# A bounded load ring, block-end states scaled in PSUM, and small zero matmuls at the start of TensorE, in a fused retention and feed-forward kernel

## The chip, the cores and the metric

The kernel runs on one core of one Trainium2 chip. The metric is the device time of one execution in microseconds. Before the change, five runs took 306.62, 307.52, 307.97, 311.42 and 312.94 us, with a median of 307.97 us. All times inside an execution are counted from the start of the span of the profiled execution.

## The reference

The inputs are q, k and v of shape (batch 8, heads 8, sequence 576, head size 64) and two weight matrices, all in float32. What is computed is a decayed causal product without softmax, then a feed-forward layer with a leaky ReLU:

```python
scores = (1/8) * q @ k.T                      # per batch and head, 576 x 576
ret    = scores * where(i >= j, gamma_h ** (i - j), 0)
x      = (ret @ v) laid out as 4608 tokens x 512
h      = x @ w_in                             # 512 x 2048
out    = maximum(0.01 * h, h) @ w_out         # 2048 x 512
```

gamma_h is 1 - 2^(-5-h) for head h.

## The kernel before

**Tiles.** The 4608 tokens are cut into 36 units of 128 tokens. A unit holds two chunks of 64 tokens; a batch has nine chunks, so units 4, 13, 22 and 31 join the last chunk of one batch with the first of the next. Per unit, q and v are scaled by powers of gamma and cast to float16 (`cast_q`, `cast_v`), and k is cast by ScalarE (`cast_k`). The scaling runs on VectorE for units 0 to 5 and on GpSimd from unit 6 (`NEARLY`). q and k are transposed on TensorE for units 0 to 8 (`transposes`, line 184, copied out of PSUM at line 190 by ScalarE for k and, from unit 4, VectorE for q), and by a DMA on SP's queue from unit 9 (`NPE`).

**Retention.** `scores(u)` makes, in one PSUM tile `sc`, the k-q products inside each chunk and the 64x64 state that each chunk adds (lines 203 and 212). `masks(u)` multiplies the products by the causal mask into SBUF. `states(u)` adds the new state to the running one on VectorE (line 243). At the last chunk of each 256-token block the sum goes first to an SBUF tile `stmp` and is then multiplied by gamma^256 (line 245). `state_copy(u)` casts the state to float16. `outputs(u)` (and `outputs_acc` for units 0 to 3) multiplies masked products by v and states by q in the PSUM tile `ot`; ScalarE and VectorE bring the result to `xT`, the transposed activations. The pools of `sc` and `ot` each hold one buffer.

**Feed-forward.** `g1_blocks(g)` makes, for a group of 256 tokens, blocks of eight matmuls (line 425) and a leaky ReLU on ScalarE (line 432). `g2_blocks` multiplies by w_out (line 448) and stores the rows through SP's queue; `g2_wide` (line 493) does the same for the first four 128-token tiles at once, in sixteen blocks.

**Order.** The order of instructions on every engine is that of the calls, written out by hand for units 0 to 8 (lines 513 to 629), and from there by `run`, which spreads steps of the retention evenly between blocks of the feed-forward. The scheduler adds only the semaphore waits. `keep_warm(n)` puts n matmuls of zeros of full size on TensorE at four places of the start.

**Loads.** k of unit 0 comes through SP's queue. All other loads of units 0 to 11 and both weight matrices are issued by GpSimd, in one queue and in this order: units 0 to 3, w_in in eight parts of half the partitions, a quarter of w_out, unit 4, a quarter of w_out, and, after some of the feed-forward's calls, unit 5, two quarters of w_out, and units 6, 7 and 8. Units 9, 10 and 11 come later in GpSimd's order, each ahead of the scaling of unit 6, 7 or 8; so a load that waits holds up the scaling behind it. The weights are cast from float32 to float16 on the way. GpSimd's DMAs use eight semaphores in turn (99 to 106 in the trace), and each DMA waits for the one eight places ahead of it to land. Loads from unit 12 on go through SP's queue.

The functions that the diff touches, with the line numbers of the profile:

Of the kernel before, what the change touches and what calls it, by code (L numbers as in the profile page):

```python
# [9 lines left out]
FP = mybir.dt.float32  # L10
F16 = mybir.dt.float16
# [6 lines left out]
def kernel(  # L18
# [23 lines left out]
    nc = tc.nc  # L42
    B, H, S, D = q.shape
    NT, DM = out.shape
    DFF = moe_w_in.shape[1]
    P = 128
    CH = 64
    BLK = 256
    NP = H // 2
    NF = DFF // P  # L50
    TOK = 512
    XR = NT // 2

    gamma = 1.0 - 2.0 ** (-5.0 - np.arange(H, dtype=np.float64))
    scale = 1.0 / np.sqrt(D)
# [22 lines left out]
    const_pool = ctx.enter_context(tc.tile_pool(name="const", bufs=1))  # L78
    ld_pool = ctx.enter_context(tc.tile_pool(name="ld", bufs=5))
    a_pool = ctx.enter_context(tc.tile_pool(name="ap", bufs=4))  # L80
# [3 lines left out]
    sc_pool = ctx.enter_context(tc.tile_pool(name="scp", bufs=1, space=PSUM))  # L84
    ot_pool = ctx.enter_context(tc.tile_pool(name="otp", bufs=1, space=PSUM))
    h_pool = ctx.enter_context(tc.tile_pool(name="hpp", bufs=2, space=PSUM))
# [15 lines left out]

    xT = const_pool.tile([P, NP, XR], F16, name="xT")
    w_in16 = const_pool.tile([P, NP, DFF], F16, name="w_in16")
    w_out16 = const_pool.tile([P, NF, DM], F16, name="w_out16")
# [15 lines left out]
    def half(i):  # L121
        return slice(CH * i, CH * i + CH)

    def kind(u):
        return kinds.index(tuple(c % CPB for b, c in units[u]))

    def load(u, x, eng):
        t = ld_pool.tile([P, H, D], FP, name=f"t32_{x}")
        t32[u, x] = t
        (b0, c0), (b1, c1) = units[u]  # L130
        src = (q, k, v)[x]
        parts = [(t, b0, c0, P)] if b0 == b1 else [(t[0:CH], b0, c0, CH), (t[CH:P], b1, c1, CH)]
        for dst, b, c, n in parts:
            eng.dma_start(  # L134
                out=dst, in_=src[b, :, CH * c : CH * c + n, :].rearrange("h t d -> t h d")
            )

    def loads(u, eng):
        for x in (1, 0, 2):
            load(u, x, eng)  # L140

    def cast_k(u):
        qk16[u] = b_pool.tile([P, 2, H, D], F16, name="qk16")
        nc.scalar.copy(out=qk16[u][:, 1], in_=t32[u, 1])  # L144

    def scaled(u, x, out):
        (nc.vector if u < NEARLY else nc.gpsimd).tensor_tensor(  # L147
            out=out,
            in0=t32[u, x],
            in1=tab_sb[:, kind(u), x // 2, :].unsqueeze(2).to_broadcast([P, H, D]),  # L150
            op=MUL,
        )

    def cast_q(u):
        scaled(u, 0, qk16[u][:, 0])
        if u >= NPE:
            qkT[u] = b_pool.tile([P, 2, NP, P], F16, name="qkT")
            nc.sync.dma_start_transpose(
                out=qkT[u].rearrange("p x c t -> p (x c) t"),
                in_=qk16[u].rearrange("t x h d -> t (x h d)"),  # L160
            )

    def cast_v(u):
        v16[u] = b_pool.tile([P, H, D], F16, name="v16")
        scaled(u, 2, v16[u])

    def casts(u):
        if u >= NU:
            return
        cast_k(u)  # L170
        cast_q(u)
        cast_v(u)

    def transposes(u, pool=None):

        qkT[u] = b_pool.tile([P, 2, NP, P], F16, name="qkT")
        if pool is None:
            trs = [y_pool.tile([P, NP, P], F16, name="yps") for x in range(2)]
        else:
            both = pool.tile([P, 2, 2 * NP, P], F16, name="sc")  # L180
            trs = [both[:, x, 0:NP, :] for x in range(2)]
        for x in (1, 0):
            for p in range(NP):
                nc.tensor.transpose(  # L184
                    trs[x][:, p, :],
                    qk16[u][:, x, 2 * p : 2 * p + 2, :].rearrange("t h d -> t (h d)"),
                    ident,
                )
        for x in (1, 0):
            (nc.scalar.copy if x or u < 4 else nc.vector.tensor_copy)(  # L190
                out=qkT[u][:, x], in_=trs[x]
            )
# [35 lines left out]
    def states(u, copy=True):  # L228

        st = sc_tiles[u][:, :, 1]  # L230
        s32 = a_pool.tile([P, 2, NP, CH], FP, name="s32")
        st32[u] = s32
        for j, (b, c) in enumerate(units[u]):
            if c == CB - 1:
                nc.vector.memset(s32[:, j], 0.0)
                continue
            ends_block = c % CPB == CPB - 1
            dst = a_pool.tile([P, NP, CH], FP, name="stmp") if ends_block else s32[:, j]
            if c == 0:
                nc.vector.tensor_copy(out=dst, in_=st[:, j])  # L240
            else:
                prev = s32[:, 0] if j else st32[u - 1][:, 1]
                nc.vector.tensor_tensor(out=dst, in0=st[:, j], in1=prev, op=ADD)  # L243
            if ends_block:
                nc.vector.tensor_tensor(
                    out=s32[:, j], in0=dst,
                    in1=gblk_sb.unsqueeze(2).to_broadcast([P, NP, CH]), op=MUL,
                )
        if copy:
            state_copy(u)  # L250

    def state_copy(u):
        st16[u] = a_pool.tile([P, 2, NP, CH], F16, name="st16")
        (nc.scalar.copy if u < NACT else nc.gpsimd.tensor_copy)(out=st16[u], in_=st32[u])  # L254
# [7 lines left out]
    def outputs_acc(u):  # L262
# [4 lines left out]
        for r in range(2):  # L267
# [11 lines left out]
            for j in range(2):  # L279
                if u == 0 and j == 0:  # L280
                    continue
                for h in (r, r + 4, r + 2, r + 6):
# [6 lines left out]
                    )  # L289
        t0 = P * u % XR  # L290
        nc.scalar.copy(
# [3 lines left out]
    def outputs(u):  # L295
# [15 lines left out]
        for j in range(2):  # L311
            for s in range(2):
                for o in range(2):
                    for g in range(2):
# [6 lines left out]
                        )  # L321
        t0 = P * u % XR
        tmp = a_pool.tile([P, NP, P], FP, name="own")
# [12 lines left out]
    FQ = DFF // 4  # L336

    def load_w_in(f):
        fs = slice(f * FQ, (f + 1) * FQ)
        rows = moe_w_in.rearrange("(o c k) f -> o k c f", o=2, k=CH)  # L340
        for o in range(2):
            nc.gpsimd.dma_start(out=w_in16[half(o), :, fs], in_=rows[o][:, :, fs])

    def load_w_out(c):
        nc.gpsimd.dma_start(
            out=w_out16[:, 4 * c : 4 * c + 4, :],
            in_=moe_w_out[c * FQ : (c + 1) * FQ, :].rearrange("(c k) f -> k c f", k=P),
        )
# [5 lines left out]
    idle = const_pool.tile([P, TOK], F16, name="idle")  # L354
    nc.vector.memset(idle, 0.0)

    def keep_warm(n):

        t = h_pool.tile([P, 1, TOK], FP, name="hps")
        for _ in range(n):  # L360
            nc.tensor.matmul(out=t[:, 0, :], lhsT=idle[:, 0:P], rhs=idle, start=True, stop=True)  # L361

    load(0, 1, nc.sync)
    load(0, 0, nc.gpsimd)
# [48 lines left out]
    def g1_blocks(g):  # L413

        tok, t0 = sizes[g], starts[g]
        nf = TOK // tok

        def block(fb):
            if fb == 0:
                g_tiles[g] = g_pool.tile([P, NF, tok], F16, name=f"gt{tok}")  # L420
            hps = h_pool.tile([P, nf, tok], FP, name="hps")
            for f in range(nf):
                fc = fb * nf + f
                for c in range(NP):
                    nc.tensor.matmul(  # L425
                        out=hps[:, f, :],
                        lhsT=w_in16[:, c, fc * P : (fc + 1) * P],
                        rhs=xT[:, c, t0 % XR : t0 % XR + tok],
                        start=(c == 0),
                        stop=(c == NP - 1),  # L430
                    )
            nc.scalar.activation(  # L432
                out=g_tiles[g][:, fb * nf : (fb + 1) * nf, :], in_=hps,
                func=mybir.ActivationFunctionType.Lrelu,
            )

        return [lambda fb=fb: block(fb) for fb in range(NF // nf)]
# [73 lines left out]
                g1[g][m]()  # L511

    g1 = [g1_blocks(g) for g in range(3)]
    casts(0)
    transposes(0)
    cast_k(1)
    scores(0)
    masks(0)
# [47 lines left out]
    def some(a, b):  # L566
        for m in range(a, b):
            wide[m]()

    g2 = g2_blocks(2)  # L570

    def more(blocks, a, b):
        for m in range(a, b):
            blocks[m]()
# [6 lines left out]
    scores(4)  # L581
    masks(4)
    states(4)
    some(5, 6)
    transposes(5, sc_pool)
    some(6, 8)
    outputs(4)
    some(8, 9)
    scores(5)
# [17 lines left out]
    casts(8)  # L607
    more(g1[2], 1, 3)
    state_copy(6)
    more(g1[2], 3, 4)  # L610
    transposes(7, sc_pool)
    more(g1[2], 4, 5)
    outputs(6)
    loads(12, nc.sync)
    casts(9)
# [4 lines left out]
    states(7, copy=False)  # L620
    more(g1[2], 7, 8)
    state_copy(7)
    casts(10)
    loads(14, nc.sync)
    more(g2, 0, 2)
    outputs(7)
    more(g2, 2, 3)
    transposes(8, sc_pool)
    more(g2, 3, 5)
    run(ends[4], g1_blocks(3), g2[5:])  # L630
    for g in range(4, NG):
        run(ends[g + 1], g1_blocks(g), g2_blocks(g - 1))
    g2 = g2_blocks(NG - 1)
    run(ends[NG], g2[:4])
    for a, b in ((0, 3 * P), (3 * P, DM)):
        y = y_pool.tile([P, DM], FP, name="yps")
        for f in range(NF):
            nc.tensor.matmul(  # L638
                out=y[:, a:b],
                lhsT=g_tiles[NG - 1][:, f, P : 2 * P],  # L640
                rhs=w_out16[:, f, a:b],
                start=(f == 0),
                stop=(f == NF - 1),
# [34 lines left out]
```

## Time and profile before

| What | Value |
|---|---|
| median of five runs (lowest, highest) | 307.97 us (306.62, 312.94) |
| profiled execution: device time | 306.62 us |
| profiled execution: span from first to last instruction | 304.8 us |
| TensorE matmuls busy | 291.8 us (96% of the span) |
| TensorE weight loads busy | 197.9 us (65%) |
| ScalarE busy | 139.7 us (46%) |
| GpSimd busy, without DMA issues' waits | 117.8 us (39%) |
| VectorE busy | 109.5 us (36%) |
| read from and written to HBM | 36.81 MB and 9.44 MB |

The profile is that of one execution. A matmul's busy time includes its way through the array, so TensorE can be shown busy while its clock is at half speed. A line of the timeline gives the start, the duration of the whole group, the engine, the line in the code, the operation, the tiles, how many instructions the group joins, and in brackets how long the engine was idle before it and what ended that. "PEld" is TensorE loading weights.

### The profile page before, as it was taken

The page shows a single profiled execution, that of the slowest core. Times are in us where ns is not written, and L with a number is a line of the kernel's source. Part 1 is how long each engine was busy: PE and PEld are TensorE (multiplying, and loading weights), DVE is VectorE, ACT ScalarE, POOL GpSimd, SP SyncE. Part 2 cuts the span into 40 slices and gives each one's busy share as a digit, 9 for nine tenths or more (in the row PEclk, how much of TensorE's full clock was granted, in tenths as well). Part 3 has the DMA queues.
Part 4 walks back from the last instruction along what each step waited for, and adds up shares of the span by engine and source line. Part 5 has one row for each costly group of instructions (what it writes and reads, how often), then busy time and mean ns, then how long its engine had stood idle before and what let it go on. Part 6 is the DMA issues. An engine that isn't in the chain of part 4 may idle for free.

```text
span 304.8 us, 9364 instructions
## 1 busy us (share of the span) xinstructions
PE 291.8 (96%) x4120; PEld 197.9 (65%) x4120; DVE 109.5 (36%) x210; ACT 139.7 (46%) x242; POOL 117.8 (39%) x142
## 2 busy tenths in 40 slices
PE   1799999999999999999999999999999999999995
PEld 1478744866766666666666666666666666666653
DVE  2750145344542425252525243424333334341001
ACT  4666634855644444444535353535353534343320
POOL 8943959944533333333333333333333330000000
PEclk9999999999999999999999999999999999999999
DMA  7999998999999997977876777767622220000111
GB/s 192 254 187 236 238 279 257 291 217 217 228 204 228 237 229 175 201 162 183 153 186 161 184 173 169 173 169 178 166 73 69 71 71 37 37 37 34 50 56 69
DMA packets 117368, 49.73 MB, mean 163 GB/s; under 512 B 106128, under 2 KB 110608, under 8 KB 117328
## 3 DMA queue, kind: packets, MB, share of 16 engines
q1 hardware_dynamic: 109760, 35.60, 50.2%
q0 software_dynamic: 7136, 13.37, 18.6%
q8 instruction: 32, 0.52, 0.7%
q10 hardware_dynamic: 432, 0.17, 0.3%
q14 instruction: 8, 0.07, 0.1%
HBM read 36.81 MB, written 9.44 MB: 152 GB/s over the span
## 4 chain that ended last, share of the span: by engine, by line
PE 93%; DVE 3%; DMA 1%; ACT 1%; issue 1%; POOL 0%; POOLq 0%; ACTq 0%
PE hps L425 41%; PE yps L448 36%; PE sc L203 3%; PE hps L493 2%; PE yps L493 2%; PE sc L212 2%; PE ot L305 2%; PE ot L316 2%; DMA t<-in_q_dram 1%; PE yps L638 1%; PE yps L184 1%; DVE s L221 1%; PE hps L361 1%; PE sc L184 1%; PE ot L272 1%
## 5 line engine op out<-in xcount | busy, mean ns | idle before, releaser
L425 PE MATMUL hps<-xT,w_in 128*128 128x256 f16 x1152 | 146.2, 273 | 0.0
L432 ACT ACTIVATE gt<-hps 128x512 f16<-128x512 f32 x144 | 86.0, 597 | 126.9 <-PE hps L425 126.8
L425 PEld LDWEIGHTS <-w_in 128*128 128x128 f16 x1152 | 112.2, 98 | 38.1
L448 PE MATMUL yps<-w_out,gt 128*128 128x512 f16 x496 | 126.6, 380 | 0.0
L254 POOL CAST st<-s 128x512 f16<-128x512 f32 x28 | 17.1, 610 | 139.2 <-DVE s L243 69.7
L448 PEld LDWEIGHTS <-gt 128*128 128x128 f16 x496 | 46.2, 98 | 33.9
L328 DVE TENSOR_TENSOR xT<-ot,own 128x512 f16<-128x512 f32 x32 | 22.1, 692 | 77.3 <-ACT own L324 77.3
L458 DVE COPY osb<-yps 128x512 f32<-128x512 f32 x31 | 21.2, 685 | 74.0 <-PE yps L448 74.0
L147 POOL TENSOR_TENSOR qk<-t,cs 128x512 f16<-128x512 f32 x30 | 31.3, 1043 | 0.1
L147 POOL TENSOR_TENSOR v<-t,cs 128x512 f16<-128x512 f32 x30 | 31.3, 1042 | 0.0
L221 DVE TENSOR_TENSOR s<-sc,cs 128x512 f16<-128x512 f32 x36 | 24.6, 683 | 8.9 <-PE sc L212 8.9
L144 ACT CAST qk<-t 128x512 f16<-128x512 f32 x36 | 22.2, 621 | 0.9 <-DMA t<-in_k_dram 0.9
L324 ACT COPY own<-ot 128x512 f32<-128x512 f32 x32 | 18.8, 586 | 7.7 <-PE ot L316 5.9
L243 DVE TENSOR_TENSOR s<-sc,s 128x256 f32<-128x256 f32 x40 | 16.8, 420 | 0.7
L203 PEld LDWEIGHTS <-qkT 64*64 64x64 f16 x576 | 8.1, 111 | 10.9 <-issue 7.8
L134 POOL DMA_DIRECT2D t<-in_q_dram x13 | 11.3, 871 | 4.5 <-DVE qkT L190 2.5
L203 PE MATMUL sc<-qkT 64*64 64x64 f16 x576 | 11.9, 203 | 1.2 <-ACT qkT L190 0.9
L134 POOL DMA_DIRECT2D t<-in_k_dram x12 | 10.4, 864 | 4.6 <-DMA t<-in_k_dram 2.3
L184 PEld LDWEIGHTS <-qk 128*128 128x128 f16 x72 | 5.5, 115 | 9.9 <-ACT qk L144 4.7
L134 POOL DMA_DIRECT2D t<-in_v_dram x13 | 11.1, 854 | 1.8 <-DMA w_in<-in_moe_w_in_dram 1.6
L184 PE MATMUL yps<-ident,qk 128*128 128x128 f16 x32 | 4.5, 309 | 7.5 <-ACT qk L144 4.7
L212 PE MATMUL sc<-v,qk 64*64 64x64 f16 x576 | 11.2, 198 | 0.0
(43 smaller groups left out, 146.1 us busy)
## 6 DMA issues: line engine op xcount, KB each, us to landing
out_dram<-osb SPq DMA_DIRECT2D x35, 256.0 KB, 2.3
t<-in_k_dram SPq DMA_DIRECT2D x22, 256.0 KB, 3.6
t<-in_q_dram SPq DMA_DIRECT2D x21, 256.0 KB, 3.9
t<-in_v_dram SPq DMA_DIRECT2D x21, 256.0 KB, 4.4
t<-in_q_dram POOLq DMA_DIRECT2D x11, 256.0 KB, 4.7
t<-in_v_dram POOLq DMA_DIRECT2D x11, 256.0 KB, 4.9
t<-in_k_dram POOLq DMA_DIRECT2D x10, 256.0 KB, 5.5
w_in<-in_moe_w_in_dram POOLq DMA_DIRECT2D x8, 256.0 KB, 9.4
```

What stands on the lines that cost most here:

```text
L134: eng.dma_start(out=dst, in_=src[b, :, CH * c : CH * c + n, :].rearrange("h t d -> t h d"))
L144: nc.scalar.copy(out=qk16[u][:, 1], in_=t32[u, 1])
L147: (nc.vector if u < NEARLY else nc.gpsimd).tensor_tensor(out=out, in0=t32[u, x], in1=tab_sb[:, kind(u), x // 2, :].unsqueeze(2).to_broadca ...
L203: nc.tensor.matmul(out=a[half(j), g, 0, p, :], lhsT=qkT[u][half(g), 1, p, half(j)], rhs=qkT[u][half(g), 0, p, half(j)], start=True, stop=T ...
L212: nc.tensor.matmul(out=a[half(g), j, 1, p, :], lhsT=qk16[u][half(j), 1, 2 * p + g, :], rhs=v16[u][half(j), 2 * p + g, :], start=True, stop ...
L221: nc.vector.tensor_tensor(out=s16s[u], in0=sc_tiles[u][:, :, 0], in1=mask_sb.unsqueeze(1).unsqueeze(1).to_broadcast([P, 2, NP, CH]), op=MUL,)
L324: nc.scalar.copy(out=tmp.rearrange("q c (j t) -> q c j t", t=CH), in_=own.rearrange("q j c t -> q c j t"),)
L328: nc.vector.tensor_tensor(out=xT[:, :, t0 : t0 + P].rearrange("q (s g) t -> q g s t", g=2), in0=far, in1=tmp.rearrange("q (s g) t -> q g s ...
L425: nc.tensor.matmul(out=hps[:, f, :], lhsT=w_in16[:, c, fc * P : (fc + 1) * P], rhs=xT[:, c, t0 % XR : t0 % XR + tok], start=(c == 0), stop ...
L432: nc.scalar.activation(out=g_tiles[g][:, fb * nf : (fb + 1) * nf, :], in_=hps, func=mybir.ActivationFunctionType.Lrelu,)
L448: nc.tensor.matmul(out=y_cur[g, tb], lhsT=g_tiles[g][:, f, tb * P : (tb + 1) * P], rhs=w_out16[:, f, :], start=(f == 0), stop=(f == NF - 1),)
L458: nc.vector.tensor_copy(out=osb, in_=y_cur[g, tb])
```

## The change

Four things change.

1. GpSimd's loads pass through `ring(size, at)`. It keeps a list of the loads issued, with their size in float32 bytes. Before a load that would bring the sum over 11 x 256 KB (2.75 MB), GpSimd copies one element of the oldest load's destination to a scratch tile, which waits for that load to land, and takes it off the list, until the new one fits.
2. At the end of a 256-token block, the sum of states is written back to its place in the PSUM tile `sc`, and is multiplied by gamma^256 from there. The tile `stmp` is gone.
3. `small_ones(60)` puts 60 matmuls of zeros, 64x64 by 64x64, ahead of everything else on TensorE, and `keep_warm(2)` is added between the transposes and the scores of unit 0.
4. The transposes of units 5, 7 and 8 use the buffer of `ot` in place of that of `sc`, and stand earlier: those of unit 5 before block 5 of `wide`, those of unit 7 one block earlier, and those of unit 8 three blocks of `g2` and `outputs(7)` earlier.

```diff
+    RING = 11 << 18
...
+    landing = []
+    probe = const_pool.tile([P, P], FP, name="probe")
+
+    def ring(size, at):
+        while landing and sum(n for n, _ in landing) + size > RING:
+            x = landing.pop(0)[1]
+            nc.gpsimd.tensor_copy(out=probe[0:1, 0:1], in_=x)
+        landing.append((size, at))
...
+            if eng is nc.gpsimd:
+                ring(H * n * D * 4, dst[0:1, 0, 0:1])
             eng.dma_start(
...
-            both = pool.tile([P, 2, 2 * NP, P], F16, name="sc")
+            both = pool.tile([P, 2, 2 * NP, P], F16, name="sc" if pool is sc_pool else "ot")
...
-            dst = a_pool.tile([P, NP, CH], FP, name="stmp") if ends_block else s32[:, j]
+            dst = st[:, j] if ends_block else s32[:, j]
...
+            ring(CH * NP * FQ * 4, w_in16[CH * o : CH * o + 1, 0, fs.start : fs.start + 1])
             nc.gpsimd.dma_start(out=w_in16[half(o), :, fs], in_=rows[o][:, :, fs])
...
+        ring(P * 4 * DM * 4, w_out16[0:1, 4 * c, 0:1])
         nc.gpsimd.dma_start(
             out=w_out16[:, 4 * c : 4 * c + 4, :],
...
+    def small_ones(n):
+        t = h_pool.tile([P, 1, TOK], FP, name="hps")
+        for i in range(n):
+            nc.tensor.matmul(
+                out=t[half(i % 2), 0, 0:CH], lhsT=idle[0:CH, 0:CH], rhs=idle[0:CH, 0:CH],
+                start=True, stop=True, skip_group_check=True,
+            )
...
+    small_ones(60)
     casts(0)
     transposes(0)
+    keep_warm(2)
     cast_k(1)
...
     states(4)
-    some(5, 6)
-    transposes(5, sc_pool)
-    some(6, 8)
+    transposes(5, ot_pool)
+    some(5, 8)
     outputs(4)
...
     state_copy(6)
-    more(g1[2], 3, 4)
-    transposes(7, sc_pool)
-    more(g1[2], 4, 5)
+    transposes(7, ot_pool)
+    more(g1[2], 3, 5)
     outputs(6)
...
     state_copy(7)
+    transposes(8, ot_pool)
     casts(10)
     loads(14, nc.sync)
     more(g2, 0, 2)
     outputs(7)
-    more(g2, 2, 3)
-    transposes(8, sc_pool)
-    more(g2, 3, 5)
+    more(g2, 2, 5)
```

## The prediction, made before the result was known

> **What bounds the kernel now.** First the page's busy table, the slices and the chain's shares by engine.
>
> ```profile
> PE 291.8 (96%) x4120; PEld 197.9 (65%) x4120; DVE 109.5 (36%) x210; ACT 139.7 (46%) x242; POOL 117.8 (39%) x142
> PE   1799999999999999999999999999999999999995
> DMA  7999998999999997977876777767622220000111
> PE 93%; DVE 3%; DMA 1%; ACT 1%; issue 1%; POOL 0%; POOLq 0%; ACTq 0%
> ```
>
> TensorE sets the end from the second slice on. Only its waits and its clock can give time back; the waits are next.
>
> ```profile
> PE yps L184 <- ACT qk L144: 4.7, 1, 4.7
> PE yps L184 <- DVE qk L147: 2.8, 2, 1.6
> PE sc L184 <- DVE s L240: 0.5, 1, 0.5
> ```
>
> 7.5 us lie at the start, while the first loads land and are cast. The third line is the only wait that the moved transposes can remove. Then the clock, from the timeline: the same two zero matmuls twice, and the places after the start where another engine may come last.
>
> ```profile
> 14.18 1.06 PE L361 MATMUL hps<-idle 128*128 128x512 f16 x2
> 20.70 0.60 PE L361 MATMUL hps<-idle 128*128 128x512 f16 x2
> 25.70 6.50 PE L425 MATMUL hps<-xT,w_in 128*128 128x256 f16 x58
> 43.05 0.61 PE L184 MATMUL sc<-ident,qk 128*128 128x128 f16 x8 [0.48 <-DVE s L240]
> 49.25 1.05 POOL L147 TENSOR_TENSOR qk<-t,cs 128x512 f16<-128x512 f32 x1
> 51.85 0.61 PE L184 MATMUL sc<-ident,qk 128*128 128x128 f16 x8
> 58.15 0.62 ACT L254 CAST st<-s 128x512 f16<-128x512 f32 x1 [0.23 <-ACT gt L432]
> 59.16 0.58 ACT L190 COPY qkT<-sc 128x512 f16<-128x512 f16 x1
> ```
>
> A 512-column matmul advances by 0.427 us at 14 us and by 0.215 us later. The trace's clock record has full speed from 20.43 us for 283.3 us. So everything before 20.43 runs at half speed.
>
> **What the Trainium skill says.** "TensorE: Matmul & The Clock Gate", Part 1: TensorE runs at half clock until one window of about 3.4 us was busy, in windows that run free. The trace agrees: 283.306 us is 83.0 windows of 3.413 us, so the window that opened the gate was 17.02 to 20.43. Part 4 of that page says that transposes do not count as busy. "DMA: Bandwidth & Descriptors", Queues, rings and completion order: each DMA engine takes a queue's descriptors in ring order. The trace agrees: GpSimd's loads land in the order of issue. "VectorE: DVE Perf Modes", Why PSUM operands drop a tier: float32 from PSUM runs at the plain rate; here a sum with a PSUM operand takes 0.41 to 0.42 us and the multiply from SBUF 0.42, so nothing is lost by the source.
>
> **Part 1, small zero matmuls.** Added: 60 of 64x64, alternating column halves. The same pattern (L272) advances in pairs every 0.053 us at half clock, so 60 take 30 x 0.053 = 1.6 us. They start when the zeros are written (VectorE, 1.04 to 1.31) and end near 3.0; the first transposes start at 4.73 when k is cast. They delay nothing. Do they open the gate? Counting array time without transposes in the trace's windows: 13.60 to 17.02 holds two keep-warm matmuls (0.85), scores (0.43) and outputs (0.86): 2.14 of 3.41 us, 63%, and did not open it. 17.02 to 20.43 holds 1.28 + 0.43 + 0.59 = 2.30 us, 67%, and did. So the threshold by this count lies near 65%. The small ones alone reach 1.6/3.41 = 47%. I take: gate not opened early, gain 0. Bound on the gain: if the 60 ran one by one (0.053 each, 3.2 us, 94% of a window that lies right), the start would run warm; what that is worth is the first rival. Bound on the loss: the window that opens the gate passes by only about 2 points, and one window later means 3.41 us at half speed over dense matmuls from 20.7, so +1.7 us.
>
> The added `keep_warm(2)` starts after the transposes of q (last start 6.75 + 0.107 = 6.86) and takes 2 x 0.427 = 0.85, to 7.71; scores of unit 0 wait for ScalarE's copy until 7.69 and started at 7.74. Cover: 0.83 us of wait. Cost 0; without that cover 0.85.
>
> **Part 2, PSUM.** There are 16 such block ends (two in each batch). In place of SBUF the sum is written to PSUM; no row shows VectorE writing PSUM. Between the PSUM copy's 0.36 and the slowest multiply shown (0.73 at 56.55) I take 0.42: no change. What moves is the release of `sc`: after the multiply, not the sum. The tightest place is unit 8: sum until 70.66, multiply 70.68 to 71.10, next scores 71.33; 0.23 us are left, and at 0.73 the wait would be 0.1. Elsewhere a unit is about 5.5 us. Cost 0 to 0.1.
>
> **Part 3, the ring.** From the landing records: the first eleven loads land 0.7 to 1.5 us apart until 14.79, the eight w_in parts at 18.11, 19.41, 20.68, 21.94, 23.22, 25.00, 25.91 and 27.20, the w_out quarters at 29.96, 36.13, 40.87 and 43.78, k, q and v of unit 6 at 44.49, 45.26 and 46.03. They come in order and without a gap, so the transfers are the limit, not the issue. Eight semaphores already hold GpSimd to eight in flight. The ring bites only where eight are more than 2.75 MB. Working it through (w_in part 0.5 MB, w_out quarter 1 MB): the sixth w_in part is issued at 18.5 in place of 14.1, the first w_out quarter at 23.6 for 18.4, the fourth at 36.5 for 33.9, k of unit 7 at 41.3 for 37.6. A load needs 3.4 us from issue to its first landing (q of unit 0: 1.27 to 4.65) when nothing is queued. 18.5 + 3.4 = 21.9 against a first landing of 22.47 before; 27.0 against 27.57; 39.9 against 40.94; for k of unit 7 44.7 against 43.95, 0.7 late, which its casts near 50 and 54 hide. So the transfers stay fed: cost 0, with 0.4 to 1.0 us to spare.
> Behind the waiting GpSimd stand the other loads and then the scaling of unit 6. From k of unit 7 on: nine issues at 0.88 from 41.3, and three one-element copies. No row shows such a copy; a 128x1 MEMSET takes 0.10 and a full CAST 0.61; I take 0.1. 41.3 + 7.9 + 0.3 = 49.5 against 49.25. Scaled q of unit 6 is then there at 50.6 in place of 50.3; TensorE asks for it at 51.85, or 51.35 after the gain below. Cover 0.8 us. The pops of units 9 to 11 add at most 9 x 0.1 over casts that TensorE needs 2 us after they end (unit 7: 54.99 against 57.0).
>
> **Part 4, the transposes.** Unit 5: its start no longer waits 0.48 us for VectorE. But `outputs(4)` now needs `ot`, which is free after the copies: state cast 43.00, k copy 43.70 to 44.29, q copy to 44.74 (VectorE follows ScalarE in every such pair of the trace). TensorE arrives at 41.65 + 0.45 + 3 x 0.865 = 44.7, starts at 44.8, before at 45.32: -0.5.
> Unit 7: from the end of `scores(6)`, now near 54.85, TensorE has 2 x 0.87 + 0.45 + 2 x 0.87 = 3.95 until `outputs(6)`: 58.8. VectorE's chain (0.69 + 0.42 + 0.42 + 0.42) ends near 57.0, the state cast near 57.9 to 58.0 (0.62, behind a leaky ReLU until 57.4), the k copy 58.6, the q copy 59.05. So a new wait of 0.3. Before, the same copies ended at 60.2 and `outputs(6)` at 59.41 waited for neither.
> Unit 8 likewise: `scores(7)` ends at 61.7, VectorE at 63.3, state cast 63.95, k copy 64.6, q copy 65.05; TensorE arrives at 61.7 + 0.87 + 0.45 + 1.73 = 64.75: 0.3.
> Sum -0.5 + 0.3 + 0.3 = +0.1, but the moved blocks are otherwise the same, and at the end of `g2`'s fifth block I get 68.1 against 68.14 before. I take -0.1; bounds -0.5 (no new wait) and +0.5 (the slow multiply in the chain).
>
> **Sum.** 0 + 0 + 0 - 0.1 on the profiled execution: span 304.7, time 306.5. That execution is the fastest of five; 306.62, 307.52 and 307.97 lie together, 307.5 in the middle, and I put the change on that: **307.4 us**, against the median shown of 307.97. About 0.5% (1.5 us) is what a measurement can tell from no change.
>
> **Rivals.** *The gate opens early.* For it: the zero matmuls sit where TensorE is otherwise idle, and one full window is enough. Against: 47%. Worth: the start cannot gain all the half-speed time, because w_in's sixth part lands at 25.00 and the matmuls that need it started at 25.77: 0.77 us, then 0.1 from the transposes. 306.6 - 0.9 = 305.7; against runs whose gate opened one window later (+1.7) more, so about 306.1 on a median of 307.97.
> *The ring starves the transfers* (slower). Place: the waits from the sixth w_in part to k of unit 7, ahead of the scaling of unit 6. Price: what the second w_out quarter's and later landings slip, less the 0.8 us of cover, plus what the following transfers lose. For it: margins of 0.4 to 1 us are thin, and a slowest engine lands 2 to 3 us after the first. Against: 2.5 MB are still queued. From a slip of 2.5 us at the third w_out quarter it decides, +1.7 or more: 309.7, to 311.
> *A later gate*, +1.7, belongs to the forecast's own spread, since before has it too.
>
> **How the numbers follow.** Forecast (nothing much) 0.50, 306.4 to 309.2 on its own; early gate 0.32; starved ring 0.18. Faster by over 0.5%: 0.75 of the early gate and 0.12 of the forecast, 0.30. Slower: 0.9 of the ring, and 0.03 of the forecast, 0.18. The rest 0.52. The range 305.5 to 309.7 leaves out half of the ring's case and a little of each other.
>
> **What would show it.** Right: 512-column zero matmuls at 0.43 us until about 20, full clock from near 20.4; no wait of transposes on VectorE at 43; waits of `ot` on line 190 of some 0.3 us near 59 and 65; w_in's sixth part landing at 25. Wrong: full clock recorded before 10 us; matmuls of line 425 waiting for w_in; the transposes of unit 6 waiting for GpSimd; the landings of w_out more than 1 us later.

## The result, and the profile after

The changed kernel took 310.24 us in the median of 43 runs (308.28 to 313.52). On the same chips the kernel before took 310.73 us in 80 runs (306.62 to 313.47). The ratio is 1.0026, with a 95% interval from 1.0007 to 1.0044. The ratio leaves out runs more than 1.5% above a kernel's own fastest; the fastest run of before is 1.7 us below that of after, so more of before's long runs fall away, and that alone puts the ratio above 1 while the medians stand the other way round. Within 0.5% the two kernels take the same time. But the fastest run became 1.7 us slower (13 of the 80 runs of before lie below the fastest of the 43), and 310.24 lies outside the range of 305.5 to 309.7.

The profiled execution after took 311.7 us, with a span of 309.1 (before 304.8). First the page's busy table, the slices of TensorE and of the DMA engines, and the chain's shares by engine.

```profile
PE 296.9 (96%) x4182; PEld 201.1 (65%) x4182; DVE 110.2 (36%) x210; ACT 139.8 (45%) x242; POOL 124.2 (40%) x181
PE   4799999999889999999999999999999999999995
DMA  7999999899899999959595867676722221000011
PE 89%; DMA 3%; DVE 2%; ACT 2%; issue 1%; SPq 1%; POOL 0%; POOLq 0%; ACTq 0%
```

TensorE still sets the end. GpSimd has 39 instructions more: the copies of the ring. DMA has 3% of the chain in place of 1%, and SP's queue ("SPq") is new in it with 1%. TensorE's waits show where:

```profile
PE yps L197 <- DVE qk L160: 2.4, 2, 1.2
PE sc L216 <- DMA qkT<-qk: 1.9, 2, 1.5
PE yps L197 <- ACT qk L157: 1.8, 2, 1.4
PE hps L382 <- DVE idle L370: 1.4, 1, 1.4
```

The second line is new: scores waited for a transpose made by DMA. The half microsecond that line 184 waited for VectorE is gone. From the timeline, in order of time: the start, the moved transposes of unit 5, the transposes of unit 6, and the wait.

```profile
1.36 1.81 PE L382 MATMUL hps<-idle 64*64 64x64 f16 x60 [1.36 <-DVE idle L370]
20.89 1.04 PE L376 MATMUL hps<-idle 128*128 128x512 f16 x2
21.72 5.47 PE L449 MATMUL hps<-xT,w_in 128*128 128x256 f16 x32
43.84 0.62 PE L197 MATMUL ot<-ident,qk 128*128 128x128 f16 x8
53.52 0.61 PE L197 MATMUL sc<-ident,qk 128*128 128x128 f16 x8
85.71 0.32 PE L216 MATMUL sc<-qkT 64*64 64x64 f16 x16 [1.53 <-DMA qkT<-qk]
```

At 20.89 two full-size zero matmuls still take 1.04 us, which is half speed, and so does most of the group of 32 matmuls of line 449. In the clock record full speed comes at 25.43 us, before at 20.43. The starts of `scores(u)` divide the 4.3 us of longer span:

| start of scores | unit 4 | 5 | 6 | 10 | 11 | 12 | 15 |
|---|---|---|---|---|---|---|---|
| before, us | 41.16 | 46.66 | 54.99 | 75.40 | 81.64 | 87.60 | 112.49 |
| after, us | 43.47 | 48.33 | 56.66 | 77.55 | 85.71 | 92.07 | 116.88 |
| difference | +2.31 | +1.67 | +1.67 | +2.15 | +4.07 | +4.47 | +4.39 |

So the later clock is +2.3, the moved transposes of unit 5 are -0.6, units 6 to 10 lose 0.5 again, and +2.2 come with scores of units 11 and 12, most of it waits for their DMA transposes (1.9). None of the four is a wait of TensorE for GpSimd. Yet the ring had moved GpSimd's work. First GpSimd's timeline of after, then that of before: the third w_out quarter, k of unit 7 and the scaling of q of unit 6.

```profile
33.65 1.35 POOL L132 COPY probe<-t 1x1 f32<-1x1 f32 x6
35.12 0.76 POOL L360 DMA_DIRECT2D w_out<-in_moe_w_out_dram  x1
37.36 0.17 POOL L132 CAST probe<-w_out 1x1 f32<-1x1 f16 x1 [1.49 <-DMA w_out<-in_moe_w_out_dram]
...
43.16 0.17 POOL L132 CAST probe<-w_out 1x1 f32<-1x1 f16 x1 [1.59 <-DMA w_out<-in_moe_w_out_dram]
43.63 0.89 POOL L147 DMA_DIRECT2D t<-in_k_dram  x1 [0.29 <-issue]
...
51.87 1.05 POOL L160 TENSOR_TENSOR qk<-t,cs 128x512 f16<-128x512 f32 x1
```

```profile
33.14 1.53 POOL L345 DMA_DIRECT2D w_out<-in_moe_w_out_dram  x2
...
49.25 1.05 POOL L147 TENSOR_TENSOR qk<-t,cs 128x512 f16<-128x512 f32 x1
```

The scaled q is ready at 52.92, before at 50.31: 2.6 us later. TensorE came for it near 53.7 (53.52, after four transposes of k), because its clock was late too, so 0.8 us were spare. In an execution whose clock opens early, they would not be. The experiments began there.

### The profile page after: what moved, and what is told of

The parts are those of the page before. It is cut to its first block, busy times and chain, and to the rows that moved or that the text cites. A ratio compares the mean times of both kernels' runs of the same rounds, so it can differ in the third digit from the quotient of the medians.

```text
span 309.1 us, 9540 instructions
## 1 busy us (share of the span) xinstructions
PE 296.9 (96%) x4182; PEld 201.1 (65%) x4182; DVE 110.2 (36%) x210; ACT 139.8 (45%) x242; POOL 124.2 (40%) x181
## 4 chain that ended last, share of the span: by engine, by line
PE 89%; DMA 3%; DVE 2%; ACT 2%; issue 1%; SPq 1%; POOL 0%; POOLq 0%; ACTq 0%
PE hps L449 39%; PE yps L472 33%; PE sc L216 3%; PE yps L517 2%; PE hps L517 2%; DMA qkT<-qk 2%; PE sc L225 2%; PE ot L318 2%; PE ot L329 1%; DMA t<-in_q_dram 1%; PE hps L376 1%; PE yps L661 1%; PE yps L197 1%; PE ot L285 1%; SPq L147 1%
## 5 line engine op out<-in xcount | busy, mean ns | idle before, releaser
L449 PE MATMUL hps<-xT,w_in 128*128 128x256 f16 x1152 | 147.9, 275 | 0.0
L329 PE MATMUL ot<-qkT,st 64*64 64x64 f16 x512 | 10.3, 194 | 0.6 <-issue 0.3
L318 PE MATMUL ot<-s,v 64*64 64x64 f16 x512 | 9.8, 194 | 0.2
```

The source lines that it names most:

```text
L449: nc.tensor.matmul(out=hps[:, f, :], lhsT=w_in16[:, c, fc * P : (fc + 1) * P], rhs=xT[:, c, t0 % XR : t0 % XR + tok], start=(c == 0), stop ...
```

## The experiments

Each ratio below is against the kernel before, on the same chip. Times are medians, with the fastest run in brackets.

### One part at a time

`ring_only` is the kernel before with the `ring` calls of the diff alone; `no_ring` is the changed kernel with `RING = 1 << 40`; `start_only` is the kernel before with `small_ones(60)` and `keep_warm(2)`. `fill_before` fills the start with full-size zero matmuls, so that the clock should open early in every execution:

```diff
+            if x and u < 2:            # in transposes, between k and q
+                keep_warm(3 + u)
...
+    keep_warm(7)                       # ahead of casts(0)
...
+    keep_warm(2)                       # after transposes(0)
...
+    keep_warm(1)
     transposes(1)
-    keep_warm(1)
+    keep_warm(2)
```

> The kernel before with the ring alone. Theory A: TensorE's clock opens by chance, early (near 20 us) in about one execution of three and late (23 to 25.5 us) in the others, whatever the change; the ring delays GpSimd's scaling of unit 6 by 2 to 2.6 us, which costs about 1.5 us in executions that open early and little in the others. Then the fastest runs are near 308.2 us in place of 306.6 to 307.5, and the middle is 0.1 to 0.4% above before. Rival B: the moved transposes, which now share the buffer of the outputs, make the loss: then this kernel equals before within 0.1%, its fastest runs included. Rival C: the small matmuls change when the clock opens: then it equals before too.

> The changed kernel with the ring's bound set so high that nothing is held back; all else of the change stays. Theory A: the loss is gone, fastest runs near 306.5 to 307, ratio to before 0.998 to 1.000. Rival B (moved transposes) and rival C (small matmuls): the loss stays, fastest runs near 308.3, ratio 1.002 to 1.003.

> The kernel before with the 60 small matmuls and the two added zero matmuls alone. Theory A and rival B: equal to before within 0.1% with both groups of times, the clock opening near 20 or from 23 to 25.5 us in the trace. Rival C: the early group of times (306.6 to 308) is missing, or the clock opens before 10 us.

> The kernel before with full-size zero matmuls (128x128 by 128x512) in every wait of TensorE from 1.36 to 11 us: 7 ahead of the first transposes, 3 between those of k and q of unit 0, 2 after them, 1 and 4 around those of k of unit 1, one more after unit 1. If the clock opens with the first window of 3.4 us that is full enough of matmuls, it opens between 4.5 and 8.5 us in every execution, and the time is near 305.8 us with little spread: w_in's sixth part still lands near 25.0, so at most 0.8 us are gained on the execution of before at 306.6, but 4 us on its late ones, about 1.3% against before's middle. If the opening hangs on something else, nothing changes.

| kernel | us (fastest) | ratio, 95% | clock full from | scaled q of unit 6 |
|---|---|---|---|---|
| ring_only | 310.23 (308.63) | 1.0004 [0.9976, 1.0032] | 19.35 | 54.25 |
| no_ring | 309.38 (306.54) | 0.9975 [0.9941, 1.0010] | 25.10 | 51.08 |
| start_only | 309.65 (306.40) | 0.9963 [0.9929, 0.9997] | 15.92 | |
| fill_before | 308.62 (306.92) | 0.9966 [0.9940, 0.9992] | 6.82 | |

The medians hardly differ; the fastest runs do. With the ring the fastest is 308.3 to 308.6, without it 306.4 to 306.9. In the profile of `ring_only`, where the clock opened at 19.35, TensorE's timeline has the wait that after's profile missed by 0.8 us:

```profile
54.31 0.40 PE L197 MATMUL sc<-ident,qk 128*128 128x128 f16 x4 [1.65 <-POOL qk L160]
```

`fill_before` opened the clock at 6.82. Its scores of unit 4 began at 40.09, 1.1 us earlier than before's. But TensorE's waits show what followed:

```profile
PE sc L205 <- DMA qkT<-qk: 3.2, 1, 3.2
```

Scores of unit 11 waited 3.2 us for the DMA transpose, and the clock record has half speed from 85.32 to 88.73, one window, soon after it. TensorE came for it about 1 us earlier than in before, and the transpose, issued at 77.48 in both, landed 2.3 us later (83.81 for 81.51). In before it had landed 0.1 us ahead of TensorE, so there was no room for either.

### The transposes' place on SP, and the bound's size

In every steady step SP issues three loads (`loads(n + 7)`) ahead of a transpose (`casts(n + 3)`). `swap_only` turns that round in the kernel before; `fill_swap` has it together with the filled start and without the ring. `fill_after` is the changed kernel with the filled start in place of the 60 small matmuls; `ring_4mb` has a bound of 4 MB.

```diff
+            casts(n + 3)
             if n + 7 < NU:
                 loads(n + 7, nc.sync)
-            casts(n + 3)
```

> The changed kernel, its 60 small matmuls replaced by the full-size zero matmuls of the kernel that opens the clock early: so the clock's chance is taken out, and ring, PSUM and moved transposes stay. Theory A (the ring costs where the start is quick): the transposes of unit 6 wait 2 us or more for GpSimd, no run below 308.3 us, median 309.5 or more, at least 0.9 us over the 308.6 of the same filling without the ring. Rival (ring harmless, its missing fast runs were the clock's chance): no such wait, median at or below 308.6, fastest near 306.5.

> The changed kernel with the ring's bound at 4 MB in place of 2.75 MB: the copies remain, most of the waits for landings go. If the loss is the transfers of w_out starved by the bound: the third quarter of w_out lands near 41 us in place of 43.0, scaled q of unit 6 is there near 51, fastest runs are back near 307, the median at 309.4 as without the ring. If it is the time that GpSimd spends in the copies: scaled q of unit 6 stays near 52 to 53, fastest runs stay at 308.3 or above.

> The kernel before, with one swap in the steady steps: the scaling and DMA transpose of unit n+3 are called before the loads of unit n+7, so that on SP's queue the transpose of unit 11 no longer stands behind three loads. If the wait of the scores of unit 11 for that transpose (0 to 3.2 us in the profiles) is what sets part of the spread, it vanishes: the transpose of unit 11 is issued near 74.5 in place of 77.5 and lands before 79, the clock no longer closes again near 85, and the median falls by 0.5 to 1.5 us to 309 to 310. If the wait only follows from the transfers' total, it stays.

> All that promises a gain together: the changed kernel without the ring's waits, with the full-size zero matmuls at the start, and with the swap of transposes and loads. Clock open by 8.5 us, no wait for GpSimd at unit 6, none for the transpose of unit 11: 305.5 to 306.5 us with a spread below 2 us, 1.3% or more below before's middle. If the wait at unit 11 stays, 308 to 309.

| kernel | us (fastest) | ratio, 95% | clock full from | scaled q of unit 6 |
|---|---|---|---|---|
| fill_after | 311.36 (308.15) | 1.0049 [1.0020, 1.0077] | 4.21 | 51.54 |
| ring_4mb | 309.41 (307.67) | 1.0001 [0.9974, 1.0028] | 24.55 | 51.90 |
| swap_only | 310.19 (306.42) | 0.9995 [0.9956, 1.0035] | 27.93 | |
| fill_swap | 306.26 (305.20) | 0.9909 [0.9875, 0.9943] | 6.60 | 50.61 |

The filled start makes the changed kernel slower. Its profile has a wait of 0.9 us for q of unit 6, then one of 2.9 us for the transpose of unit 11, then a window at half speed (86.13 to 89.55):

```profile
PE sc L218 <- DMA qkT<-qk: 2.9, 1, 2.9
...
PE sc L197 <- POOL qk L160: 0.9, 1, 0.9
```

`ring_4mb` keeps 34 of the 39 copies. Its third w_out quarter landed at 41.52 in place of 43.04, and its median is that of `no_ring` (309.41 and 309.38), as expected if the waits for landings cost most; its fastest run, 307.67, came only part of the way to the 307 expected.
The same start together with the swap and without the ring is faster than both kernels: `fill_swap` is 4.3 us below before and 4.0 below after, by the medians. Its profile has no wait at unit 11. The swap alone gains nothing that can be measured, where 0.5 to 1.5 us were expected; its profiled execution was one of its longest (312.42 us), with the latest clock of all and an idle stretch of 1.7 us on TensorE at 19.9 to 21.6 that no releaser explains.

### The ring, with chance taken out

With the filled start and the swap the clock was full from 4 to 7 us in each profile whose record shows it, so a part's cost can be read directly. `fs_ring` is `fill_swap` with the ring of 2.75 MB. `fs_base` is the kernel before with filled start and swap. `fs_again` and `fs_third` are `fill_swap` again, beside the others on their chips. `before_again` is one more execution of the kernel before. In `fs_copies` the ring's 39 copies stay in their places but read a constant, so that none waits for a landing and nothing is held back by one. `fs_moves` is `fs_base` with the moved transposes only.

```diff
-            nc.gpsimd.tensor_copy(out=probe[0:1, 0:1], in_=x)
+            nc.gpsimd.tensor_copy(out=probe[0:1, 0:1], in_=idle[0:1, 0:1])
```

> The changed kernel with its ring, its small matmuls replaced by the full-size zero matmuls, and with the swap of transposes and loads: both chances (clock, transpose of unit 11) are taken out, the ring stays. If the ring costs by holding up GpSimd ahead of the scaling of unit 6: 0.9 to 2.5 us over the same kernel without the ring's waits (306.3), so 307.2 to 308.8, with a wait of the transposes of unit 6 for GpSimd of that size. If the ring is harmless: 306.3 within 0.3.

> The kernel before with the full-size zero matmuls and the swap: no ring, and also no scaling in PSUM and no moved transposes. Against the kernel that has these two parts besides (306.3): by the traces so far the moved transposes take 0.5 us off unit 5 and give some of it back in waits for the buffer of the outputs, so 306.3 to 306.8. If they cost more than they give, 305.8 to 306.2.

> The kernel with full-size zero matmuls, swap, PSUM scaling and moved transposes, without the ring's waits, once more beside the two others on one chip: 306.3, all runs from 305 to 308.

> The kernel before once more, for a second profile. Theory A: with two chances in three the clock opens from 23 to 25.5 us; then the scores of unit 4 come near 43.5 in place of 41.2, and the time is 309 to 311. With one in three it opens before 20.5, and the time is 306.5 to 308. A clock that opens late with a time under 308, or early with over 309 and no wait at unit 11, would speak against it.

> The changed kernel with the full-size zero matmuls at the start and the transposes' issue ahead of the loads, with the ring's GpSimd copies at the same places and in the same number, but each copy reads a constant tile, so no copy waits for a load and no load is held back. If the ring costs through its waits for landings, this stands within 0.5 us of the kernel without a ring (305.6 to 306.3 us) and the scaled q of unit 6 ends near 50.1 to 50.5 us of the profile. If it costs through GpSimd's own time in the copies (some 27 to 39 of 0.17 to 0.23 us), that q ends near 51.5 to 52 and the time is near 308.5, as with the ring whole.

> The kernel before with the full-size zero matmuls at the start and the transposes' issue ahead of the loads, and the moved transposes of units 4 and later; states scaled as before, not in PSUM, and no ring. If the moved transposes carry the 0.7 to 1.3 us that the two parts together gained, this equals the kernel with both (305.6 to 306.3). If the scaling in PSUM carries it, this equals the kernel with neither (306.9).

> The changed kernel without its ring, with the full-size zero matmuls and the transposes' issue ahead of the loads, once more, as the reference on the same chip for the other two: 305.6 to 306.3 us.

| kernel | us (fastest), runs | ratio, 95% | third w_out quarter issued, landed | scaled q of unit 6 | from scores 5 to scores 6 |
|---|---|---|---|---|---|
| fs_base | 306.94 (305.76), 10 | 0.9903 [0.9870, 0.9936] | landed 40.95 | 50.09 | 8.33 |
| fs_again | 305.61 (305.03), 6 | 0.9885 [0.9830, 0.9940] | landed 41.02 | 50.11 | 8.33 |
| fs_ring | 308.58 (306.31), 22 | 0.9953 [0.9928, 0.9978] | 36.05, 41.94 | 52.07 | 9.82 |
| fs_third | 305.48 (305.16), 6 | 0.9855 [0.9815, 0.9895] | 32.80, 40.35 | 49.48 | 8.33 |
| fs_copies | 306.35 (306.00), 6 | 0.9870 [0.9835, 0.9904] | 34.98, 40.81 | 51.30 | 9.61 |
| fs_moves | 305.49 (305.17), 6 | 0.9833 [0.9803, 0.9864] | 33.33, 41.87 | 51.00 | 8.50 |

(`before_again`: 307.4 us in its one run, clock full from 19.82.)

**The ring costs 2.3 to 3.0 us** once TensorE is early: 308.58 against 306.26 and 305.61. In the profile of `fs_ring` it is the wait for q of unit 6:

```profile
PE sc L197 <- POOL qk L160: 1.3, 1, 1.3
```

TensorE's timeline of `fs_copies`, then that of `fs_third`:

```profile
49.85 0.39 PE L197 MATMUL sc<-ident,qk 128*128 128x128 f16 x4
51.35 0.40 PE L197 MATMUL sc<-ident,qk 128*128 128x128 f16 x4 [1.11 <-POOL qk L160]
```

```profile
50.02 0.61 PE L197 MATMUL sc<-ident,qk 128*128 128x128 f16 x8
```

So the copies alone, with no wait for a landing, bring a wait of 1.1 us back. The median is 0.87 us above that of `fs_third`, the fastest run 0.84; with six runs each the intervals of the two ratios overlap, so it is the wait in the profile that shows the cost, and not the times. My expectation was that one cause would carry nearly everything; neither does. GpSimd's timeline of `fs_copies` shows the copies ahead of the third quarter; that of `fs_third` has the third and fourth quarter in one line:

```profile
33.05 1.86 POOL L132 CAST probe<-idle 1x1 f32<-1x1 f16 x6
34.98 0.76 POOL L362 DMA_DIRECT2D w_out<-in_moe_w_out_dram  x1
```

```profile
32.80 1.53 POOL L362 DMA_DIRECT2D w_out<-in_moe_w_out_dram  x2
```

Six copies take 1.86 us, the quarter is issued 2.2 us later than in `fs_third`, and the fourth lands at 44.62 in place of 42.95. So does what follows: k of unit 6 lands at 45.28 for 43.71, the load eight places behind it waits for that landing, and the scaling of q stands behind that load. In `fs_ring`, which has the waits for landings too, the issue is at 36.05 and q another 0.8 us later. The rest of the 2.2 us between the medians of `fs_ring` and `fs_copies` is not one place in a profile. In 12 of the 22 runs of `fs_ring` the mean granted clock was below 0.996, in 6 of 26 of its counterparts without a ring; one window at half speed lowers it by 0.5 x 3.41 / 305 = 0.006. The runs at clock 1.000 had a median of 307.7 with the ring, of 306.2 with the copies alone, and of 305.3, 305.4 and 305.8 without a ring (`fs_again`, `fs_third`, `fill_swap`). That an idle TensorE behind the ring's wait is what loses these windows is likely and not shown: no such run was profiled.

**The moved transposes carry the gain, PSUM none.** `fs_moves` stands at 305.49, with both parts at 305.48. At its own place the gain is small: from scores of unit 4 to scores of unit 9 `fs_base` takes 30.18 us, `fs_moves` 29.90, `fs_third` 29.92. The medians differ by 1.3 to 1.5 us, more than the 0 to 0.5 expected, the fastest runs by 0.6 to 0.7. In the profile of `fs_base` most of the rest is a wait for the DMA transpose of unit 10, which `fs_moves` has not:

```profile
PE sc L205 <- DMA qkT<-qk: 1.4, 1, 1.4
```

Whether the moves remove it is open: `fs_again`, which has them, waited 0.7 us at the same place.

## Why the prediction was wrong, step by step

**Sum: the level was wrong, and it made most of the error.** I took 307.5 us as the ordinary time of before, from three of five runs lying together. Of 80 runs 17 lie below 308.6, and the median is 310.73, 3.2 us above my level; the whole miss is 2.8. Against that level the forecast was a change of -0.1, and the measurement is -0.5 in the medians and +0.8 (0.26%) in the ratio. The profile I summed over was the fastest of the 80. Both profiles of before (306.62 and 307.4 us) are of early executions, so what fills its ordinary 310.7 us was never seen. A late clock fits: executions with nearly the same start that opened it at 24.55 to 27.93 us took 308.3 to 312.4 (`ring_4mb`, `no_ring`, after, `swap_only`). It is not the only way to such a time: `ring_only` opened at 19.35 and took 311.1.

**Part 1: right that the small ones do nothing, wrong in the measure of the clock.** The 60 took from 1.36 to 3.0 us, as worked out, and opened nothing there: full speed came at 15.92 in `start_only` and at 25.43 after. (The interval of `start_only` ends just short of 1, but over all of its runs the mean is 0.1% below that of before.) But my count of array time without transposes, with a threshold near 65%, falls with after's window from 18.60 to 22.01: 84% by that count, and it did not open the clock. I had dropped the transposes on the word of the Trainium skill ("TensorE: Matmul & The Clock Gate", Part 4), which says that they don't count as busy "the same way"; I took that as not at all. What comes nearest is to keep them and to weight each matmul by the share of the array it fills, a quarter for 64x64. Before's window that opened: 0.70 us of transposes, 1.28 of full-size zeros and 0.70 weighted of small ones, 2.68 / 3.41 = 79%. After's nearest miss, 15.19 to 18.60: 0.85 + 0.85 + 0.85 = 2.55, 75%; and the one that broke my count has 71%. This count isn't exact either: the window that opened the clock in `start_only`, 12.51 to 15.92, has 74%. But without transposes after's miss at 71% stands above before's opener at 58%, so to leave them out is wrong here. Which window passes depends on the phase of the free-running windows, as Part 1 of that page says; the price of missing, which I put at +1.7 for one window, was +2.3 in after's profile (25.43 for 20.43; the phase differed too).

The rival *The gate opens early* was priced well: with a filled start scores of unit 4 began at 39.8 to 40.6, 0.5 to 1.4 us before those of before's profile (41.16), against 0.9 forecast, and w_in became the limit as said (0.9 us of waits in `fill_before`). It only needed full-size matmuls.

**Part 2: right.** The sum into PSUM took 0.432 us in all 16 cases and the multiply 0.424 to 0.425; it moved nothing.

**Part 3 failed: "a load needs 3.4 us from issue to its first landing" and "cover 0.8 us".** 3.4 us was q of unit 0, a load of 256 KB of plain float32 (0.5 MB is read in a w_in part, 1 MB in a w_out quarter, and both are cast). The first two w_out quarters took 5.0 us to their first landing (23.96 to 29.01, 29.41 to 34.42; the second still had six loads of 256 KB or less ahead of it, so its 5.0 us are not all its own). The first came 1.8 us after the last of w_in had landed (27.18), where before 0.4 us lay between them (27.20, 27.57): the queue that I took as fed ran dry. Both first landings were then 1.4 us late, and by the end the third quarter landed 2.2 us late and the fourth 1.8 (43.04 for 40.87, 45.60 for 43.78). A copy took 0.17 us and, with six in a row, 0.22 to 0.31 each, not 0.1; after one that had waited, another 0.28 passed before the next issue. q of unit 6 came at 52.92 and not at 50.6. That the cover came out at 0.8 us in after's profile is luck: TensorE slipped as far as q did (its transposes of unit 6 began at 53.52, where 51.35 was forecast). The cover was read from an execution that need not be the earliest, and it was less than nothing in each early one with the ring (waits of 1.6, 1.3 and 0.9 us in `ring_only`, `fs_ring` and `fill_after`).
The rival *The ring starves the transfers* had the place right and its price near: 2.2 us of slip against 2.5 from which it was to decide, 2.3 to 3.0 us of cost against 1.7 or more. It was wrong on when it shows: the wait for q of unit 6 comes in early executions and is hidden where the clock is late. `no_ring` beats after by 0.9 in the median and by 1.7 in the fastest run.

**Part 4: right in mechanism and size.** Unit 5 gained 0.6 (0.5 forecast), and the new waits ahead of `outputs(6)` and `outputs(7)` cost 0.2 each (0.3 forecast: from scores 6 to 7 it is 6.83 us for 6.65, from 7 to 8 7.64 for 7.47). From unit 4 to unit 9 that is -0.2 against the -0.1 of the forecast.

**Not in the prediction: the DMA transposes of units 9 to 12.** SP's timeline, after and then before; the first line of each is unit 9, the second unit 11:

```profile
65.03 1.64 SPq L171 DMA_TRANSPOSE qkT<-qk  x1
...
80.68 3.05 SPq L171 DMA_TRANSPOSE qkT<-qk  x1
```

```profile
61.68 2.69 SPq L158 DMA_TRANSPOSE qkT<-qk  x1
...
77.48 2.02 SPq L158 DMA_TRANSPOSE qkT<-qk  x1
```

The transpose of unit 11 was issued 3.2 us later, while TensorE was only 2.2 us late, and landed at 85.67. I had not followed SP's queue past the ring's loads. SP's order alone is enough for such a wait: it is 3.2 us in `fill_before`, without a ring, and gone in `fs_ring`, with the ring and the swap. But the ring very likely has a part in it. The transpose of unit 9 needs q of unit 9, which GpSimd scales, and that q was ready at 61.66 in before and at 65.00 in after. Without filled start and swap, both profiles with the ring of 2.75 MB (after, `ring_only`) take 14.5 us from scores of unit 10 to scores of unit 12; those without it (before, `before_again`, `start_only`, `no_ring`) take 12.2 to 12.7, and `ring_4mb` 12.3. So in after's profile, against that of `no_ring` with a clock as late, the ring shows as 1.8 us here and not at unit 6. These are single profiles; how often it happens is open.

Together: how the ring's cost, the moves' small gain and the two chances, clock and transpose, end near zero in the median is not shown. The median of `ring_only`, with the ring and nothing else, is that of before (310.23 and 310.49). In the fastest run, where the ring is bare, they end at +1.7.

## What to carry to other kernels

Before a wait is costed at nothing, ask how the cover behaves in the earliest execution, not in the one that was profiled, and use the latency of a transfer of the same size and kind. Where the clock opens by chance, five runs don't give a level: fill the start with full-size matmuls in the compared kernels first, and small costs become readable. When TensorE gains at the start, look for the next thing that it then reaches too early, here a queue whose transposes stand behind loads.

## What the runs showed of the hardware

- One kernel, the same before, opened its clock at 19.82 and 20.43 us in two profiles, variants of the same start at 15.92 to 27.93. With the start filled it was 4.0 to 7.1 us in every profile whose record shows it.
- An idle stretch of 3.2 us (`fill_before`) and of 2.9 us (`fill_after`) each cost one window of 3.41 us at half speed; 1.53 us (after) did not. Of each of the two, 1.94 us lay in the window that ended as half speed began (81.91 to 85.32 and 82.72 to 86.13), and 1.53 us was the most idle time in any recorded window that full speed outlasted. The Trainium skill ("TensorE: Matmul & The Clock Gate", Why this matters for your kernels) asks for no gap above about 3 us; here 2.9 was already enough.
- A copy of one element on GpSimd took 0.17 us, a fifth of the issue of a q, k or v load (0.88), and the 33 of 39 that stand ahead of the scaling of unit 6 made TensorE wait 1.1 us for it (`fs_copies`).
